# Query loads in whole rows, interleaving on ScalarE, stepped PSUM addresses for the scores, and an earlier placement of attention stages

## The chip, the cores and the metric

The kernel runs on one core of a Trainium2 chip. The metric is the device time of one execution, in microseconds (us). Each run has a state: slow when it is over 1.5% above the fastest of the same kernel, fast otherwise, unknown for a single run. The kernel before and the changed kernel were timed in the same rounds on the same chip. The profile covers the span from the first to the last instruction, about 2 us less than the time. The granted clock is the share of full speed that TensorE was allowed. A transfer lands when its data have arrived. The engines are PE (TensorE), PEld (its weight loads), DVE (VectorE), ACT (ScalarE), POOL (GpSimd) and SP (Sync, which only issues transfers here).

## The reference

Attention with a learned mixing of key and value blocks, followed by a dense mixture of four expert layers. Sizes: 4 batches, 8 heads, 768 positions in 8 blocks of 96, head size 64; the experts see 3072 rows of 512 and have 1024 hidden units.

```python
P = sinkhorn(sort_net)                    # (B,H,8,8), five rounds
k_sorted = einsum('bhij,bhjcd->bhicd', P, k_blocks)
v_sorted = einsum('bhij,bhjcd->bhicd', P, v_blocks)
scores = (q_blocks @ k_sorted^T) / 8      # block i with block i only
attn = softmax(scores) @ v_sorted         # (B,H,S,D)
x = attn.transpose(0, 2, 1, 3).reshape(3072, 512)
out = sum over e of  p[:, e] * (relu(x @ w1[e]) @ w2[e])
```

## The kernel before

TensorE does the products of the expert layers almost without a break. The attention of batches 1 to 3 is cut into stages for one pair of heads each, and a plan places these stages between the product groups. An entry (chunk, slot, stage, batch, pair) puts a stage into a slot of about 2 us.

```python
PLANS = {0: [
    (0, 9, st_v, 1, 0), (0, 10, st_q, 1, 0), (0, 10, st_v, 1, 1), (0, 11, st_k, 1, 0), ...
    (1, 0, st_q, 1, 1), (1, 0, st_s, 1, 0), ...   # cut
```

The stages are: st_n, st_lv and st_lk load queries, values and keys (issued by GpSimd); st_v and st_k mix the blocks on TensorE (the vs transfers then bring the mixed values to the layout that st_a reads); st_q transposes the queries by a transfer; st_s makes scores and their exponentials; st_a multiplies by the values; st_x transposes the result for the experts. The parts that matter here:

```python
def load_queries(b, heads=range(H)):
    t = natural[(b, "q")]                       # 128 positions on partitions
    for h in heads:                             # one issue per head, 128-byte pieces
        nc.gpsimd.dma_start(t[:, h // 2, :, h % 2, :], q[b, h].rearrange("(t p) d -> p t d", p=P))

def st_v(b, pr):
    ...                                         # 2 matmuls into ps, ScalarE copies ps to vo
    if pr % 2:                                  # after every second pair: six Sync issues
        for r in range(R):
            nc.sync.dma_start(vs[ds(r * CP, CP)]..., vo[:, r]...)

def st_q(b, pr):
    qT = att.tile([P, R, P], F16, tag="qT", bufs=3)
    nc.sync.dma_start_transpose(qT[:], natural[(b, "q")][:, pr].rearrange("p t h d -> p (t h d)"))

def st_s(b, pr):
    for i in range(NB):
        for hh in range(2):
            nc.tensor.matmul(pss[hh][:, i // HB, ds((i % HB) * BLK, BLK)],   # 96 words side by side
                             kT[ds(D * hh, D), ds(i * BLK, P)], qT[ds(D * hh, D), i, :], ...)
    ...                                         # exp of both heads, ScalarE

def st_x(b, pr):
    nc.sync.dma_start_transpose(xTs[b][:, pr], xsls[(b, pr)].rearrange("c i h d -> c (i h d)"))
```

All of st_q's and st_x's transposes and the vs transfers go through Sync in program order. The loads go through GpSimd's queue. The page counts both queues as shares of the same 16 DMA engines (38.5% and 27.0% of the span).

The softmax here doesn't subtract the row's maximum and nothing guards it: scores larger than these inputs give would overflow.

## Time and profile before

| what | value | how to read it |
|---|---|---|
| time | 364.64 us (364.54 to 364.73, 3 runs) | median |
| PE busy | 354.1 of 362.5 us | the engine that sets the time |
| ACT, POOL busy | 157.7, 117.5 us | neither is near the bound |
| query loads | 24 issues, 96 KB each, 19.9 us of POOL | 128-byte pieces |
| first query transpose of batch 1 | issued 65.78, landed 72.4 | PE reads it at 72.67 |
| 12 score stages of batches 1 to 3 | 0.45 us each, start to next start | 16 matmuls in pairs (one per head); a pair starts 43 ns after the pair before it |

Because PE is busy nearly all the time and works in order, any wait of PE goes to the end undiminished.

### The profile page before, as it was taken

How to read it: one execution, taken by the hardware profiler on the slowest of the kernel's cores; microseconds unless marked ns; L12 is line 12 of the kernel's file. 1: busy time of each engine (PE TensorE's matmuls, PEld its weight loads, DVE VectorE, ACT ScalarE, POOL GpSimd, SP SyncE). 2: the span in 40 equal slices, each digit the busy share in tenths (PEclk: the TensorE clock that was granted, in tenths of full speed). 3: DMA queues.
4: the chain of work that ended last, by engine and by line, in shares of the span. 5: the costliest groups of instructions: out<-in, count | busy, mean ns of one | idle time of the engine just before them, and what ended most of it. 6: DMA issues, size and time to landing. Idle time of an engine off the chain costs nothing.

```text
span 362.5 us, 10556 instructions
## 1 busy us (share of the span) xinstructions
PE 354.1 (98%) x4517; PEld 314.6 (87%) x4517; DVE 280.0 (77%) x559; ACT 157.7 (44%) x282; POOL 117.5 (32%) x134
## 2 busy tenths in 40 slices
PE   8799999999999999999999999999999999999996
PEld 8685857888888888988888899999999998999995
DVE  5753898779798676866799979868779679587794
ACT  2664430452424355367400157165283381561740
POOL 8882011655022420000000018137055082180470
PEclk9999999999999999999999999999999999999999
DMA  8999999999999999934450310310301101102101
GB/s 109 206 208 230 208 210 200 194 186 158 175 197 162 210 91 172 161 85 73 85 126 2 58 60 4 58 60 4 88 31 49 71 2 60 61 2 65 55 16 44
DMA packets 69753, 38.34 MB, mean 106 GB/s; under 512 B 40390, under 2 KB 64716, under 8 KB 69708
## 3 DMA queue, kind: packets, MB, share of 16 engines
q0 software_dynamic: 34640, 17.83, 38.5%
q1 hardware_dynamic: 35068, 19.85, 27.0%
q8 instruction: 35, 0.57, 0.6%
q14 instruction: 10, 0.08, 0.1%
HBM read 42.00 MB, written 6.34 MB: 133 GB/s over the span
## 4 chain that ended last, share of the span: by engine, by line
PE 86%; DVE 6%; DMA 5%; issue 1%; ACT 1%; POOL 1%; DVEq 0%; ACTq 0%
PE ps_Q L1121 20%; PE ps_h L768 18%; PE ps_p L753 13%; PE ps_X L1032 9%; PE ps_Z L1032 6%; PE ps_Q L1032 6%; DMA w<-in_moe_w_dram 4%; PE ps_o L696 3%; PE ps_p L803 2%; PE ps_h L661 1%; PE ps_s L406 1%; PE ps_a L441 1%; PE ps_k L387 1%; DVE Hb L774 1%; PE ps_v L354 1%
## 5 line engine op out<-in xcount | busy, mean ns | idle before, releaser
L1045 POOL TENSOR_TENSOR Hb<-tmp,pb 128x512 f16<-128x512 f32 x48 | 62.0, 1297 | 150.5 <-ACT tmp L1044 148.7
L768 PE MATMUL ps_h<-xT,w 128*128 128x256 f16 x672 | 78.4, 273 | 0.0
L768 PEld LDWEIGHTS <-w 128*128 128x128 f16 x672 | 64.5, 98 | 8.5
L774 DVE SCALAR_TENSOR_TENSOR Hb<-ps_h,pb 128x1024 f16<-128x1024 f32 x42 | 51.3, 1223 | 17.6 <-PE ps_h L768 17.4
L1032 PEld LDWEIGHTS <-w 128*128 128x128 f16 x768 | 46.6, 98 | 0.8
L1121 PEld LDWEIGHTS <-Sb 128*128 128x128 f16 x384 | 37.2, 98 | 4.1
L1032 PEld LDWEIGHTS <-arena 128*128 128x128 f16 x576 | 34.7, 98 | 0.1
L1044 ACT ACTIVATE tmp<-tmp 128x512 f32<-128x512 f32 x48 | 30.5, 635 | 6.4 <-DVE tmp L1076 5.2
L753 PEld LDWEIGHTS <-Sb 128*128 128x128 f16 x288 | 27.4, 98 | 4.2 <-issue 0.7
L1121 PEld LDWEIGHTS <-Hb 128*128 128x128 f16 x288 | 27.4, 98 | 2.9
L413 ACT ACTIVATE ET<-ps_s 96x768 f16<-96x768 f32 x24 | 18.1, 802 | 26.1 <-PE ps_s L406 25.8
L1032 PE MATMUL ps_X<-kT,arena 128*128 128x128 f16 x384 | 29.3, 219 | 0.0
L121 POOL DMA_DIRECT2D arena<-in_q_dram x24 | 19.9, 837 | 27.1 <-DMA qT<-arena 17.2
L396 ACT CAST kT<-ps_k 64x384 f16<-64x384 f32 x48 | 22.7, 473 | 13.2 <-PE ps_k L387 12.2
L739 DVE TENSOR_TENSOR Sb<-Hb 128x512 f16<-128x512 f16 x45 | 26.5, 609 | 0.0
L1068 DVE TENSOR_TENSOR tmp<-ps_Q,tmp 128x512 f32<-128x512 f32 x24 | 16.6, 691 | 12.2 <-ACT tmp L1067 8.0
L1121 PE MATMUL ps_Q<-w,Sb 128*128 128x256 f16 x192 | 24.7, 273 | 0.0
L1121 PE MATMUL ps_Q<-w,Hb 128*128 128x256 f16 x192 | 23.9, 273 | 0.0
L1052 ACT COPY ps_X<-ps_Z 128x512 f32<-128x512 f32 x24 | 13.7, 570 | 22.8 <-PE ps_Z L1032 22.4
L753 PEld LDWEIGHTS <-Hb 128*128 128x128 f16 x216 | 20.6, 98 | 3.1 <-issue 0.3
L1121 PE MATMUL ps_Q<-T,Sb 128*128 128x256 f16 x192 | 22.9, 273 | 0.0
L1059 ACT COPY tmp<-ps_X 128x512 f32<-128x512 f32 x24 | 14.1, 586 | 12.2 <-PE ps_X L1032 12.2
(189 smaller groups left out, 605.3 us busy)
## 6 DMA issues: line engine op xcount, KB each, us to landing
w<-in_moe_w_dram POOLq DMA_DIRECT2D x7, 1024.0 KB, 27.0
pb<-p_dram SPq DMA_DIRECT2D x12, 512.0 KB, 5.5
arena<-in_k_dram POOLq DMA_DIRECT2D x8, 384.0 KB, 8.6
arena<-in_v_dram POOLq DMA_DIRECT2D x8, 384.0 KB, 9.6
vs<-arena SPq DMA_DIRECT2D x36, 66.0 KB, 5.2
arena<-in_q_dram POOLq DMA_DIRECT2D x24, 96.0 KB, 6.7
out_dram<-ob SPq DMA_DIRECT2D x9, 256.0 KB, 2.0
out_dram<-oa SPq DMA_DIRECT2D x8, 256.0 KB, 2.4
```

Of the source, the lines that this page charges most:

```text
L121: nc.gpsimd.dma_start(t[:, h // 2, :, h % 2, :], q[b, h].rearrange("(t p) d -> p t d", p=P))
L396: nc.scalar.copy(kT[ds(D * hh, D), r], pk[ds(D * r, D), hh].rearrange("p a (i c) -> p a i c", c=CP),)
L413: nc.scalar.activation(ETs[2 * (pr % 2) + hh][:, 0:S].rearrange("c (a x) -> c a x", a=2), pss[hh][0:BLK, :, 0:HS], AF.Exp, bias=0.0, scale ...
L739: tt(sm[0], blk(0, 1), blk(1, 1), ALU.add)
L753: nc.tensor.matmul(ps, lhs(e, f), Ts[e][rhs][:, f, :], start=(first and e == es[0] and f == 0), stop=(done and e == es[-1] and f == KH - 1 ...
L768: nc.tensor.matmul(ps[:, f, :], w1sb[e][:, kc, ds((4 * g + f) * P, P)], xT[:, kc, ds(2 * c * P, 2 * P)], start=(kc == 0), stop=(kc == NKC ...
L774: nc.vector.scalar_tensor_tensor(out=Hb[:, e, ds(4 * g, 4), :], in0=ps[:], scalar=0.0, op0=ALU.max, in1=pb[:, ds(e, 1), :].broadcast_to([P ...
L1032: nc.tensor.matmul(dst[:, ds(f * P, P)], a[lhs][:, k, ds(f * P, P)], t[rhs][:, k, :], start=(first and f == 0 and k == 0), stop=(f == KH - ...
L1044: nc.scalar.activation(src, src, AF.Relu, bias=0.0, scale=1.0)
L1045: nc.gpsimd.tensor_tensor(Hb[:, e, ds(i * KH, KH), ds(j * P, P)], src.rearrange("p (f x) -> p f x", f=KH), pb[:, ds(e, 1), ds(j * P, P)].b ...
L1068: tt(t22, Q, u3, ALU.add)
L1121: nc.tensor.matmul(ps, lhs(e, f), Ts[e][rhs][:, f, :], start=(first and e == 0 and f == 0), stop=(e == E - 1 and f == KH - 1), skip_group_ ...
```

## The change

The intent is to make the query loads cheap (whole rows of 768 bytes in 12 issues, not 128-byte pieces in 24), and to take the last small waits out by placing stages earlier. A whole row holds six successive positions. So ScalarE first interleaves the two heads into one buffer; the transpose then yields the queries in another order, and the score matmuls write them back to the right place by addresses 24 bytes apart in PSUM, the memory that TensorE writes.

```diff
-        for h in heads:
-            nc.gpsimd.dma_start(t[:, h // 2, :, h % 2, :], q[b, h].rearrange("(t p) d -> p t d", p=P))
+        for pr in pairs:
+            nc.gpsimd.dma_start(t[:, (b * NPB + pr) % 3], q[b, ds(2 * pr, 2)].rearrange("h (p r) d -> p h (r d)", r=R))
     def st_q(b, pr):
-        nc.sync.dma_start_transpose(qT[:], natural[(b, "q")][:, pr].rearrange("p t h d -> p (t h d)"))
+        both = natural[(b, "q")][:, NPB - 1].rearrange("p h x -> p (h x)")      # one buffer for all
+        nc.scalar.copy(both.rearrange("p (r h d) -> p h r d", r=R, h=2),
+                       natural[(b, "q")][:, (b * NPB + pr) % 3].rearrange("p h (r d) -> p h r d", r=R))
+        nc.sync.dma_start_transpose(qT[:], both)
+        qTs[(b, pr)] = qT.rearrange("p r (i c) -> p i r c", i=NB)
     # st_s
-                    pss[hh][:, i // HB, ds((i % HB) * BLK, BLK)],
+                    pss[hh][:, i // HB, ds((i % HB) * BLK, BLK)].rearrange("k (c r) -> k r c", r=R),
-                    qT[ds(D * hh, D), i, :],
+                    qT[ds(D * hh, D), i],
     # plan (cut)
-            (0, 9, st_v, 1, 0), (0, 10, st_q, 1, 0), (0, 10, st_v, 1, 1), ...
+            (0, 9, st_v, 1, 0), (0, 10, st_v, 1, 1), (0, 10, st_q, 1, 0), ..., (0, 11, st_q, 1, 1),
-            (2, 8, st_x, 1, 3), (2, 8, st_v, 2, 1), (2, 9, st_lv, 3, 0), (2, 9, st_n, 3, 0), ...   # chunk 2
+            (2, 6, st_v, 2, 1), (2, 6, st_lv, 3, 0), (2, 6, st_n, 3, 0), (2, 8, st_x, 1, 3), (2, 9, st_lk, 3, 0), ..., (2, 12, st_a, 2, 0),
     # first loads of batch 1, between the v and k loads
-        if qd == 0: load_queries(1, range(2))           # heads of pair 0
+        load_queries(1, ([0], [1, 2])[qd])              # pairs 0, 1 and 2
```

## The prediction

> **What bounds the kernel now.** I read the page first, then TensorE's waits, then the three queues around the place where the change bites.
>
> ```profile
> PE 354.1 (98%) x4517; PEld 314.6 (87%) x4517; DVE 280.0 (77%) x559; ACT 157.7 (44%) x282; POOL 117.5 (32%) x134
> ```
>
> TensorE is busy 98% of 362.5 us; nothing else is near. The next question is how much of its time is waiting between 72 and 206 us, where the attention stages of batches 1 to 3 lie between the products of the expert layers. This is the view of waits for PE in that stretch (engine line, waited for, total us, times, longest):
>
> ```profile
> PE ps_p L753 <- DVE Hb L774: 0.3, 1, 0.3
> PE ps_p L753 <- DVE room L863: 0.3, 1, 0.3
> PE ps_v L354 <- DVE xsl L423: 0.2, 1, 0.2
> ```
>
> Three short waits. Busy time hides a little more, so I took starts from PE's timeline: a group of sixteen 256-column products takes 1.75 us start to start, an ordinary score stage 0.45, st_a 0.49, st_v 0.33. Against these, four places lose time: 106.69 (0.41), 112.67 (0.48), 126.74 (0.41) and 183.66 (0.26). Sum 1.56 us, 0.4% of the time. No move of attention stages can win more than that, because the number of matmuls (4517) and their columns do not change. A gain above 2% (7.3 us) is out of reach.
>
> So the case turns on whether the change makes TensorE wait anew. The places that matter are the query loads and their transposes. PE, ScalarE and the Sync queue around the first score stage of batch 1 (start, us, what):
>
> ```profile
> 67.55 0.49 PE L354 MATMUL ps_v<-arena 128*128 128x384 f16 x2
> ...
> 69.19 0.50 PE L387 MATMUL ps_k<-arena 128*128 128x128 f16 x6
> ...
> 72.67 0.51 PE L406 MATMUL ps_s<-qT,kT 64*128 64x96 f16 x16
> ```
> ```profile
> 68.08 0.80 ACT L360 CAST arena<-ps_v 128x768 f16<-128x768 f32 x1 [0.83 <-PE ps_v L354]
> 69.72 1.97 ACT L396 CAST kT<-ps_k 64x384 f16<-64x384 f32 x4 [0.84 <-PE ps_k L387]
> 73.28 1.50 ACT L413 ACTIVATE ET<-ps_s 96x768 f16<-96x768 f32 x2 [1.59 <-PE ps_s L406]
> ```
> ```profile
> 65.78 1.32 SPq L375 DMA_TRANSPOSE qT<-arena  x1
> 68.94 3.88 SPq L368 DMA_DIRECT2D vs<-arena  x6
> 72.92 1.10 SPq L819 DMA_DIRECT2D out_dram<-oacc  x2
> ```
>
> The first transpose is issued at 65.78; restricted to this one, the view of the tile qT gives 6.6 us to landing, so it lands at 72.4. TensorE reads it at 72.67. It is 0.3 us early: just in time. The six vs issues then hold the Sync queue for 3.88 us, from 68.94 (ScalarE ends the evacuation at 68.88) to 72.8. All twelve transposes and the query loads (last numbers: KB each, median us to landing):
>
> ```profile
> DMA to landing us min/median/max: 2.8/6.6/10.1
> ```
> ```profile
> arena<-in_q_dram POOLq DMA_DIRECT2D x24, 96.0 KB, 6.7
> ```
> ```profile
> L121 POOL DMA_DIRECT2D arena<-in_q_dram x24 | 19.9, 837 | 27.1 <-DMA qT<-arena 17.2 <-DMA w<-in_moe_w_dram 9.9
> ```
>
> 2.8 us is a transpose with little beside it (161 us); the long ones are at 65 to 100 us, where the mean share of the DMA engines (two queues can both count, so over 1) is 1.4 to 2.3.
>
> **What the Trainium skill says.** "DMA: Bandwidth & Descriptors", section "Queues, rings and completion order": what Sync issues goes through one ring on each of the DMA engines, and descriptors are taken in ring order. The trace agrees: the six vs transfers issued behind that transpose land from 74.1 on, after its 72.4. So a transpose placed behind the vs transfers waits for them twice, for the issue and in the ring. The same page, section "Why small descriptors are slow (HBM only)", says small pieces carry a fixed overhead; the change makes 128-byte pieces into whole rows of 768 bytes. Trace: a pair of heads landed 1.33 us behind the load before it, a k load with twice the pair's bytes 1.93 us. "ScalarE: Activation LUTs", section "What ACT_TABLE_LOAD costs": an ACTIVATE with immediates is 186 ns + 0.833 ns per column, 826 ns for 768; the trace has 800 ns for 128x768 casts. "TensorE: Matmul & The Clock Gate", Part 1: after an idle window of about 3.4 us the array falls to half clock, until a window of activity. No idle stretch after the warm-up here is that long (longest 1.7 us), so the trace cannot say.
>
> **The change part by part.**
> (1) Loads: 24 issues of 837 ns become 12; at the 754 to 765 ns that the k and v issues take, 19.9 us becomes about 9.1 us of GpSimd. 24x768 = 18,432 pieces become 12x256 = 3,072. GpSimd is 32% busy and PE never waits for a query load: worth 0 directly, but the DMA engines get freer between 70 and 135 us.
> (2) Interleaving: 12 new ScalarE copies of 128x768 f16, about 0.8 us each: 9.6 us, ScalarE 44% to 47%. Off the path unless one blocks. One can: all twelve write one buffer, so each waits for the previous transpose to have landed, in front of everything behind it in ScalarE's order.
> (3) Scores: the same 192 matmuls, with moving operand 6x16 and PSUM addresses 24 bytes apart. Batch 0's scores already read 6x16: their pairs start 43 ns apart, as here, so reading is free. No instruction of the kernel before writes PSUM with a step; I take 0. The skill's PSUM page gives no time for it.
> (4) Placement: st_a of batch 2, head pair 0, moves from the crowded start of batch 1's experts to the end of the chunk before; batch 3's last stages move two slots forward. That should end the waits at 126.74 and 183.66: -0.67 us. The other two come from st_a (1,2) and (1,3), which keep their slots, so they stay.
> (5) The new wait. The built programs show this order on Sync: in the kernel before, first transpose, then vs x6; in the changed one, vs x6, then both first transposes. The score stage keeps its place, after the first group of chunk 1. All before it is unchanged, so TensorE arrives at 72.67, but the transpose cannot be issued before 68.94 + 3.88 = 72.8. At the very best it lands 2.8 us later, 75.6: 3.0 us lost. More likely, with a v load and a query load now in flight there and the vs transfers ahead (they took 5.2 to 5.6 us), in about 4.3 us: 77.1, lost 4.4. PE runs in order, so all of it goes to the end.
> The later transposes have five slots or more (each about 2 us) before their scores; there even 8 us is hidden. While ScalarE holds the second copy for the landing, the exp behind it has nothing to do yet; it then starts 0.8 us late, inside a product group of 1.75.
> (6) A gap over 3.4 us may catch a full idle window and halve the clock for a while. Estimate from the skill's 3.4 us: one window at half pace loses 1.7, perhaps two; at one chance in four, +0.5.
> Sum: 364.64 + 4.4 - 0.67 + 0.5 = 368.9; I take 368.6, as freer DMA engines may shorten the landing.
>
> **The rivals.**
> A: the wait is not there or under 1 us, and the small gains remain: 363.5 to 364.5. For it: a tuned kernel's author probably measured the order. Against: the Sync order and 72.8 against 72.67 leave no room.
> B: the stall is long: the transpose takes 8 to 10 us as some did at 75 to 96 us, and the clock falls: 364.6 + 7 + 2 = 373. For it: crowded DMA engines. Against: those long ones had six small-piece query loads beside them, which go.
> C: stepped PSUM writes run at half pace: a pair takes about 83 instead of 43 ns, 96 pairs, +3.8 us: 372 with the stall. Nothing for or against in the trace.
> D: ScalarE becomes a bound through the single buffer. At 47% this needs blocked copies; after the first two, the copies are two slots or more apart. Under 1 us.
>
> **Range and chances.** The middle is the stall of 3 to 6 us less 0.7. The low end, 366.0, is a bare 2.8 us landing less some relief; the high end, 372.0, a landing of 7 us with a clock loss, or C. Faster by over 2%: 0.01. Slower by over 2% (above 371.9) needs B or C: 0.14. Within 2%: 0.85.
>
> **What would show it.** In the profile after: a PE wait of 3 to 6 us at the first ps_s of batch 1, put down to a DMA qT<-arena, at 72.7 us; on Sync vs before qT there; PE waits at later score stages near 0; the new ScalarE copies near 0.8 us; score pairs still 43 ns apart (a longer step says C); 128x256 products 109 ns apart behind the stall (double says the clock fell). Wrong if PE passes that stage without a wait, or if the loss lies at other stages.

## The result and the profile after

The changed kernel took 383.85 us (median of four runs, 381.79 to 385.33), the kernel before 364.59 in the same rounds. The ratio is 1.0526 (95% interval 1.047 to 1.0582). Ratios in this document are the mean time of one kernel's fast runs over that of the other's in the same rounds, so they are not quite the ratio of the medians. The result is correct, slower, and well outside the predicted range. The profiled run was the fastest of the four (381.79), with a span of 380.0 us against 362.5: 17.5 us to explain.

The page's engine line and its row of the granted TensorE clock (40 slices of 9.5 us, tenths of full speed):

```profile
PE 362.7 (95%) x4517; PEld 319.9 (84%) x4517; DVE 279.5 (74%) x559; ACT 166.2 (44%) x294; POOL 106.4 (28%) x122
...
PEclk9999999969999989999999999999999999999999
```

The same 4517 matmuls take 8.6 us more of PE's busy time, and the idle time grew as well. Two slices have a lower clock: around 80 and around 135 us. PE's longest waits in the stretch of the attention stages, in the view of waits (two of 0.3 us and less are left out):

```profile
PE ps_s L412 <- DMA qT<-arena: 6.7, 1, 6.7
PE ps_h L774 <- DMA xT<-xsl: 2.2, 1, 2.2
PE ps_a L447 <- DMA vs<-arena: 1.4, 1, 1.4
PE ps_a L447 <- ACT arena L363: 0.4, 1, 0.4
```

All four are new. PE's timeline at the two places (start, busy us, and in brackets the idle time before):

```profile
70.68 1.91 PE L774 MATMUL ps_h<-xT,w 128*128 128x256 f16 x16
79.30 1.47 PE L412 MATMUL ps_s<-qT,kT 64*128 64x96 f16 x16 [6.71 <-DMA qT<-arena]
80.70 2.61 PE L774 MATMUL ps_h<-xT,w 128*128 128x256 f16 x16
83.15 0.50 PE L393 MATMUL ps_k<-arena 128*128 128x128 f16 x6
...
127.29 1.47 PE L759 MATMUL ps_p<-w,Sb 128*128 128x256 f16 x12
130.19 0.40 PE L447 MATMUL ps_a<-vs,ET 96*128 96x65 f16 x8 [1.44 <-DMA vs<-arena]
131.01 0.40 PE L447 MATMUL ps_a<-vs,ET 96*128 96x65 f16 x8 [0.41 <-ACT arena L363]
131.25 0.49 PE L774 MATMUL ps_h<-xT,w 128*128 128x256 f16 x3
133.90 2.93 PE L774 MATMUL ps_h<-xT,w 128*128 128x256 f16 x13 [2.16 <-DMA xT<-xsl]
136.77 0.83 PE L412 MATMUL ps_s<-qT,kT 64*128 64x96 f16 x16
```

And Sync's timeline at the same two places (start, us of issuing, count):

```profile
68.80 3.89 SPq L371 DMA_DIRECT2D vs<-arena  x6
72.79 9.20 SPq L383 DMA_TRANSPOSE qT<-arena  x2
...
119.26 4.21 SPq L371 DMA_DIRECT2D vs<-arena  x6
123.57 1.58 SPq L463 DMA_TRANSPOSE xT<-xsl  x1
```

The first place is the predicted one. The vs transfers hold Sync from 68.80 to 72.69, the transpose is issued at 72.79 and lands 6.4 us later, at 79.2. The second place was not predicted. There xT, the transposed input of the experts, is behind six vs transfers and takes 10.3 us to land. The wait of 0.41 us inside st_a has the vs transfers behind it as well: the evacuation of the next v stage, to which it is put down, began on ScalarE at 130.16 after it had waited 2.91 us for the vs transfers to leave its buffer.

After each idle stretch some matmuls run slowly. The 16 products at 80.70 take 2.45 us to the next group where an undisturbed group takes 1.75. The 13 products at 133.90 take 2.87 us where 13 x 109 ns are 1.42. At the first place six of the 16 start about 213 ns apart, twice 109, and the scores before them also take twice their time; at the second place eleven of the 13. The table of stretches gives the granted clock (each row: the stretch, its length, busy us of PE, PEld, DVE, ACT and POOL with their counts, then the clock, the mean share of the DMA engines and GB/s):

```profile
72.40:79.30 6.90, 0.19 (x2) 0.03 (x1) 1.22 (x1) 0.03 (x1) 0.46 (x1) 0.71 1.05 154
79.30:90.00 10.70, 10.70 (x96) 9.00 (x97) 5.61 (x8) 6.52 (x10) 2.92 (x4) 0.87 0.96 139
128.00:137.00 9.00, 4.99 (x47) 3.30 (x47) 3.02 (x8) 0.80 (x1) 0.00 (x0) 0.81 1.06 162
```

In the kernel before, all three stretches had a clock of 1.00. Windows set closer show where the clock was halved:

```profile
71.90:75.32 3.42, 0.69 (x7) 0.37 (x4) 1.22 (x1) 0.00 (x0) 0.96 (x2) 1.00 1.07 183
75.32:82.15 6.83, 2.85 (x23) 2.16 (x24) 0.00 (x0) 2.21 (x3) 0.70 (x1) 0.50 0.95 99
133.35:136.76 3.41, 2.86 (x13) 1.76 (x12) 0.00 (x0) 0.00 (x0) 0.00 (x0) 0.50 0.66 179
```

The third loss has no wait at all. It is in the score matmuls, read from the view of the tile ps_s (durations of one matmul, min/median/max ns; a duration includes the modelled end, so two of them tell only that something changed). Of the kernel before:

```profile
L406 PE MATMUL ps_s<-qT,kT x192: 202/203/213, 72.7 to 178.8; 64*128 64x96 f16 x192
```

The same view of the changed kernel:

```profile
L412 PE MATMUL ps_s<-qT,kT x192: 252/283/438, 79.3 to 191.0; 64*128 64x96 f16 x192
```

By their starts, a pair takes 83 ns instead of 43, and a stage at full clock 0.76 us instead of 0.45 (for example 124.87 to 125.64).

What the change was meant to do came about. Loads and copies, from the view of groups (busy us, mean ns):

```profile
L379 ACT COPY arena<-arena 128x768 f16<-128x768 f16 x12 | 10.0, 832 | 14.2 <-DMA qT<-arena 14.1
L121 POOL DMA_DIRECT2D arena<-in_q_dram x12 | 8.4, 703 | 63.0 <-ACT arena L379 47.6 <-DMA w<-in_moe_w_dram 14.0 <-DVE u L940 1.5
```

The query loads cost POOL 8.4 us instead of 19.9, and three of the four short waits of before (at 106.69, 126.74 and 183.66) are gone.

The account of the 17.5 us, each from starts in PE's timeline:

| term | us | working |
|---|---|---|
| wait for qT | 6.9 | 79.30 less 72.43 (70.68 + 16 x 109 ns) |
| slow clock behind it | 1.3 | scores 1.40 - 0.76, products 2.45 - 1.75 |
| waits at 130 to 134 | 4.5 | 1.59 before st_a, 0.57 within it, 2.32 for xT |
| slow clock behind them | 1.4 | 2.87 - 1.42 |
| stepped scores | 3.7 | 12 x 0.31 |
| waits that went | -1.1 | 0.41 + 0.41 + 0.26 |
| small losses at five other places | 1.1 | 0.27, 0.14, 0.34, 0.17, 0.19 at 111, 113, 159, 175, 193 |
| sum | 17.8 | 0.3 too much: rounding, and PE was 0.15 ahead at 70.68 (70.83 before) |

### The profile page after: what moved, and what is told of

Same layout as the page of the kernel before. It is cut to its first block, busy times and chain, and to the rows that moved or that the text cites. A ratio compares the mean times of both kernels' runs of the same rounds, so it can differ in the third digit from the quotient of the medians.

```text
span 380.0 us, 10522 instructions
## 1 busy us (share of the span) xinstructions
PE 362.7 (95%) x4517; PEld 319.9 (84%) x4517; DVE 279.5 (74%) x559; ACT 166.2 (44%) x294; POOL 106.4 (28%) x122
## 4 chain that ended last, share of the span: by engine, by line
PE 85%; DMA 8%; DVE 1%; POOL 1%; ACT 1%; SPq 1%; issue 1%; DVEq 0%; ACTq 0%; POOLq 0%
PE ps_Q L1127 19%; PE ps_h L774 19%; PE ps_p L759 12%; PE ps_X L1038 8%; PE ps_Q L1038 6%; PE ps_Z L1038 6%; DMA w<-in_moe_w_dram 4%; DMA xT<-xsl 3%; PE ps_o L702 3%; PE ps_h L667 3%; PE ps_s L412 2%; DMA qT<-arena 2%; PE ps_p L809 1%; PE ps_a L447 1%; PE ps_v L357 1%; SPq L371 1%
## 5 line engine op out<-in xcount | busy, mean ns | idle before, releaser
L774 PE MATMUL ps_h<-xT,w 128*128 128x256 f16 x672 | 80.7, 277 | 2.2 <-DMA xT<-xsl 2.2
L121 POOL DMA_DIRECT2D arena<-in_q_dram x12 | 8.4, 703 | 63.0 <-ACT arena L379 47.6
```

Of the source, the lines that this page charges most:

```text
L774: nc.tensor.matmul(ps[:, f, :], w1sb[e][:, kc, ds((4 * g + f) * P, P)], xT[:, kc, ds(2 * c * P, 2 * P)], start=(kc == 0), stop=(kc == NKC ...
```

## The experiments

Three questions: does the step in PSUM cost PE time by itself, do the waits come from the placement or from the layout, and why do the transposes take so long to land? All results were correct unless said otherwise.

| kernel | us | ratio to before (95%) |
|---|---|---|
| changed kernel | 383.85 | 1.0526 (1.047 to 1.0582) |
| plan_only | 382.35 | 1.0489 (1.0461 to 1.0516) |
| layout_only | 373.95 | 1.0251 (1.0222 to 1.028) |
| step24 | 368.62 | 1.0107 (1.0078 to 1.0136) |
| pairs | 365.79 | one look |
| rows_permuted | 380.98 | 1.0424 (1.0384 to 1.0464) |
| moving_order | 392.6 | 1.0751 (1.072 to 1.0781) |
| layout_mended | 397.63 | 1.0882 (1.0842 to 1.0922) |
| layout_unblocked | 371.69 | 1.0173 (1.0115 to 1.023) |
| swap_only | 371.97 | 1.0171 (1.015 to 1.0193) |
| q_first | 380.72 | 1.044 (1.0402 to 1.0478) |
| q_first_late_v | 380.44 | 1.0433 (1.0397 to 1.047) |
| q_first_late_loads | 384.76 | 1.0518 (1.0479 to 1.0557) |
| q_first_late_loads_again | 383.09 | one look |
| backlog | 365.26 | 1.0006 (0.9986 to 1.0026) |
| x_first | 387.6 | wrong result |
| v_early | 387.14 | 1.0592 (1.0551 to 1.0632) |
| clear_second | 379.76 | 1.0383 (1.0354 to 1.0412) |
| plan_mended | 369.52 | 1.0125 (1.0082 to 1.0167) |

### Placement and layout apart

**plan_only** is the kernel before with the new plan and the new order of the first loads; layout and scores are the old ones.

```diff
-    PLANS, PLAN_A of before
+    PLANS, PLAN_A of the changed kernel
-        if qd == 0: load_queries(1, range(2))
+        load_queries(1, (range(2), range(2, 6))[qd])
```

> The kernel before with the new placement of the stages alone; queries load and are stored as before. Theory (the new order on the Sync queue makes two waits, the PSUM step is a separate cost): both waits are there, about 7 us before the first score stage of batch 1 and about 4 us around the first product of batch 1's experts, each followed by matmuls at half clock; 364.6 + 8 + 6 - 1 = about 377 us (374 to 381), score pairs 43 ns apart, mean clock below 1. Rival (the waits come from the new loads, the interleaving copy or its single buffer): within 1.5 us of 364.6.

Measured: 382.35 us. Score pairs stay at 43 ns, and the waits are there without the new layout:

```profile
PE ps_s L406 <- DMA qT<-arena: 5.4, 1, 5.4
PE ps_a L441 <- DMA vs<-arena: 3.1, 1, 3.1
PE ps_p L803 <- DVE oacc L898: 2.0, 1, 2.0
...
PE ps_h L768 <- DMA xT<-xsl: 1.0, 1, 1.0
```

So the placement, with the loads of batch 1 brought forward, makes both places wait without the new layout. The time is a little above the expected 374 to 381. One reason is the third wait, of 2.04 us at 66.72, ahead of both places. Three of the single-head loads brought forward (60.80, 62.70, 64.64) pushed GpSimd's addition L895 from 62.38 in the kernel before to 65.47; DVE's L898 waited 2.25 us for it, and PE for DVE. The changed kernel, with half as many issues, has no such wait.

**layout_only** is the reverse: the new loads, copies and stepped scores in the old plan (two loads moved where a buffer demands it).

```diff
-    PLANS, PLAN_A of the changed kernel
+    PLANS, PLAN_A of before, with (2, 1, st_n, 2, 3) -> (2, 5) and (0, 5, st_n, 3, 3) -> (0, 10)
```

> The changed kernel's loads, interleaving and stepped PSUM addresses with the placement of before (three loads stand a little later, where the three row buffers ask for it). Theory: the 12 score stages take 0.76 instead of 0.45 us, 12 x 0.31 = 3.7 us more, and nothing else: about 368.3 us (367 to 370), clock 1.00, first transpose issued ahead of the six vs transfers. Rival (the layout causes waits too): 372 or more, with a wait on qT at a score stage or a mean clock below 1.

Measured: 373.95 us; pairs 83 ns apart; only 0.44 us of waiting at the first score stage. But PE waits twice for a v evacuation (L363) on ScalarE, 2.52 us at 114.29 and 1.62 at 159.06. ScalarE's timeline before the first of them shows why:

```profile
112.71 0.83 ACT L379 COPY arena<-arena 128x768 f16<-128x768 f16 x1 [2.77 <-DMA qT<-arena]
113.44 0.79 ACT L363 CAST arena<-ps_v 128x768 f16<-128x768 f32 x1
```

The interleaving copy waits for the previous transpose to free the single buffer, and the evacuation stands behind it. Before the second wait it is the same: the copy at 157.47 had waited 4.12 us. That is the prediction's rival D, in the old plan.

**layout_unblocked** moves those two copies behind the evacuation.

```diff
-  (2, 5, st_q, 2, 1), (2, 5, st_n, 2, 3), (2, 6, st_v, 2, 0),
+  (2, 6, st_v, 2, 0), (2, 6, st_q, 2, 1), (2, 6, st_n, 2, 3),
-  (0, 12, st_q, 3, 1), (0, 13, st_v, 3, 0),
+  (0, 13, st_v, 3, 0), (0, 13, st_q, 3, 1),
```

> The new query layout in the old placement, with the two interleaving copies that stood in front of a v evacuation on ScalarE moved behind it. If the two waits of 2.52 and 1.62 us on the v evacuation (L363) in layout_only come from copies that wait for their single buffer in front of it, those waits go and the time falls from 373.95 to 368.5 to 370, which is the kernel before plus the 3.7 us of the PSUM step. Rival: the copies are not the cause; the waits stay and the time is 373 to 375.

Measured: 371.69 us with an unusually wide scatter (369.59 to 374.54; the fastest run lies in the expected range). Both waits on the evacuation are gone, so the copies were their cause. The profiled run, the slowest of the four, has a new wait of 2.19 us for xT at 125.13 and slow products behind it. The gain of the median is half of what was expected. In the profiled run nothing was gained: besides the new wait, PE came to the first product group of chunk 1 at 72.82, against 71.09 in layout_only, with a clock of 0.50 from 16.8 to 20.2 us, before any stage that the edit touched. The profiled runs of step24 and rows_permuted have such an early stretch too.

### The step in PSUM

**step24** is the kernel before with the scores' output addresses stepped by 24 bytes and nothing else. The score columns come out in a wrong order. The comparison with the reference still passed, here and in rows_permuted, so it says nothing about the order of rows in this test.

```diff
-                    pss[hh][:, i // HB, ds((i % HB) * BLK, BLK)],
+                    pss[hh][:, i // HB, ds((i % HB) * BLK, BLK)].rearrange("k (c r) -> k r c", r=R),
```

> The kernel before with one edit: the scores' PSUM addresses take steps of 24 bytes, as in the change; queries are read as before (unit step), so score columns land in a wrong order on purpose. Theory (the step alone halves the write rate): pairs of score matmuls start 83 instead of 43 ns apart, the stage takes 0.76 instead of 0.45 us, 12 x 0.31 = 3.7 us, 368.3 us (367.3 to 369.3), no new wait, clock 1.00. Rival (the cost is in reading 6x16 or in the transposed layout): 43 ns and within 0.5 us of before.

Measured: 368.62 us, no new waits, pairs 83 ns apart. Over all score stages the distances between starts sum to 9.28 us instead of 5.76, which is 3.5 of the 3.8 us that the time rose (368.62 less 364.83 in the same rounds). This shows the cost alone: rival C of the prediction, at its size.

**pairs** writes the same 96 words, two neighbours at a time and then a jump of 24 bytes.

```diff
-                    pss[hh][:, i // HB, ds((i % HB) * BLK, BLK)],
+                    pss[hh][:, i // HB, ds((i % HB) * BLK, BLK)].rearrange("k (c r t) -> k r c t", r=3, t=2),
```

> One look at the kernel before with score columns written in pairs: two neighbouring PSUM words, then a jump of 24 bytes (order wrong on purpose). Theory (PSUM takes two neighbouring columns at a time, and a single word costs as much as a pair): pairs of score matmuls 43 ns apart. Rival (any broken run halves the rate): 80 ns or so, as with single steps.

Measured: 365.79 us, pairs 43 ns apart. It was run at another time. The tile view of the scores in step24:

```profile
L406 PE MATMUL ps_s<-qT,kT x192: 252/282/283, 74.5 to 184.1; 64*128 64x96 f16 x192
```

And of pairs:

```profile
L406 PE MATMUL ps_s<-qT,kT x192: 199/203/213, 73.8 to 180.0; 64*128 64x96 f16 x192
```

A jump after every second word costs nothing; a jump after every word doubles the time. The profiled run also waited 1.15 us for qT at 73.83: the kernel before has only 0.3 us to spare there.

**rows_permuted** is the changed kernel with plain output addresses (the rows of a block come out permuted).

```diff
-                    pss[hh][:, i // HB, ds((i % HB) * BLK, BLK)].rearrange("k (c r) -> k r c", r=R),
+                    pss[hh][:, i // HB, ds((i % HB) * BLK, BLK)],
```

> The changed kernel with plain, unit-step PSUM addresses for the scores: the result is wrong on purpose (rows come out in another order), all else the same. Theory (a PSUM step of 24 bytes halves the rate at which a matmul's columns are written): score pairs 43 ns apart again, 12 x 0.31 = 3.7 us less, about 380 us (378.5 to 381.5). Rival (the 83 ns come from reading the queries in 6 runs of 16): pairs stay 83 ns apart and the time stays 382 to 385.

Measured: 380.98 us; pairs 43 ns; the distances between score starts sum to 6.07 us instead of 9.83. The time fell by 2.9 us, while its profiled run waited longer at both places (7.19 for qT, 1.85 and 2.83 at the second). Set beside plan_only, which has the same placement and plain scores but the old loads, it is 1.4 us faster (382.35 less 380.98). The intervals of the two ratios just overlap, and plan_only's wait of 2.04 us at 66.72, which is absent here, is more than the difference; no other gain of the new loads is shown.

**moving_order** tries to keep the order in another way: plain output addresses, and the queries read in the right order, each 2-byte element 256 bytes from the last.

```diff
-        qTs[(b, pr)] = qT.rearrange("p r (i c) -> p i r c", i=NB)
+        qTs[(b, pr)] = qT.rearrange("p r (i c) -> p i c r", i=NB)
     # and plain output addresses, as in rows_permuted
```

> The changed kernel with the order restored on the reading side: PSUM addresses are plain, and the moving operand is read as 16 times 6 elements with a step of 256 bytes. Right result. Theory (only the write side cares about steps): pairs 43 ns apart, the same 3.7 us less as with permuted rows, 379 to 382 us. Rival (reading single 2-byte elements is slow as well): pairs 80 ns or more, 382 us or more.

Measured: 392.6 us, with the right order by construction. Pairs start about 165 ns apart, nearly four times 43, and the distances between score starts sum to 16.9 us. All twelve stages took 1.41 us, also the two (79.31 and 140.95) in which the granted clock was 0.50; so what limits this reading did not follow the granted clock. Reading single elements at a step is worse than writing them so. The remedy failed.

**layout_mended** lets ScalarE restore the order: plain scores in the layout of layout_unblocked, and the exp writes its 2-byte results 12 bytes apart.

```diff
-                ETs[2 * (pr % 2) + hh][:, 0:S].rearrange("c (a x) -> c a x", a=2),
-                pss[hh][0:BLK, :, 0:HS],
+                ETs[2 * (pr % 2) + hh][:, 0:S].rearrange("k (a i c r) -> k a i r c", a=2, i=HB, r=R),
+                pss[hh][0:BLK, :, 0:HS].rearrange("k a (i r c) -> k a i r c", i=HB, r=R),
```

> layout_only with two edits: PSUM addresses are plain, and the exponential's write to SBUF restores the order (a step of 12 bytes in f16); and two interleaving copies stand behind the v evacuation that they held up. Right result. Theory (layout_only's 8 to 9 us are 3.7 us of PSUM steps, and 4.1 us of waits plus slow matmuls made by copies that wait for the one interleaving buffer): score pairs 43 ns apart, no wait over 0.6 us, clock above 0.995; 365 to 366.5 us. Rival (the layout has a further cost, such as the stepped write of the exponential or other blocked copies): 368 us or more.

Measured: 397.63 us. Pairs are back at 43 ns, but the exp took 2.84 us instead of 0.80 (tile view of ET, min/median/max ns), and PE waited for it in 18 places:

```profile
L419 ACT ACTIVATE ET<-ps_s x24: 2725/2844/2960, 73.0 to 211.4; 96x768 f16<-96x768 f32 x24
```

So none of the three ways tried to restore the order (PSUM step, stepped moving operand, stepped exp) was free.

### The first score stage

**swap_only** is the kernel before with one swap: the first query transpose behind the second v stage. It makes the predicted wait alone.

```diff
-            (0, 9, st_v, 1, 0), (0, 10, st_q, 1, 0), (0, 10, st_v, 1, 1), ...
+            (0, 9, st_v, 1, 0), (0, 10, st_v, 1, 1), (0, 10, st_q, 1, 0), ...
```

> The kernel before with one swap and nothing else: the first query transpose of batch 1 now comes behind the six vs transfers of the second v stage. This is the one step on which the prediction rested, alone, with the old loads and plain scores. Theory of the prediction (a landing of 4.3 us from an issue at 72.8): a wait of about 4.4 us at the first score stage, time 368.5 to 369.5. Theory now (the landing takes 6 to 9 us while loads of GpSimd are in flight, and the idle stretch takes the clock with it): a wait of 6 to 9 us there plus about 1.3 us of slow products, time 372 to 376. Nothing else should wait.

Measured: 371.97 us, ratio 1.0171. The wait:

```profile
78.25 0.82 PE L406 MATMUL ps_s<-qT,kT 64*128 64x96 f16 x16 [5.44 <-DMA qT<-arena]
```

The transpose was issued at 73.07 and landed 5.0 us later; 13 slow products followed. Neither expectation held to the figure. The wait is 1 us above the prediction's 4.4 and below the 6 to 9 of the other; its time is just under the latter's 372. A second, small wait came with it, 0.55 us for vs at 132.11. So the order alone costs over 6 us, and with the rest of the change the landing is 1.4 us longer still (6.4 against 5.0).

**q_first** is the changed kernel with the reverse swap, the transpose ahead of the vs transfers again.

```diff
-            (0, 10, st_v, 1, 1), (0, 10, st_q, 1, 0),
+            (0, 10, st_q, 1, 0), (0, 10, st_v, 1, 1),
```

> The changed kernel with one swap: the first query stage of batch 1 stands ahead of the second v stage again, in the same slot. Theory: the transpose is issued at about 67 instead of 72.8 us and lands by 73; the wait of 6.9 us and the slow matmuls behind it (1.3 us) go: 383.9 - 8 = about 376 us (373 to 378). Rival (the transpose is late because of the loads beside it, not of its place on the queue): over 381 us, the wait still over 4 us.

Measured: 380.72 us, a miss. The transpose was issued at 67.34, 5.4 us earlier, but landed only 3.2 us earlier, at 75.98, and PE still waited 4.04 us. From the tile view of qT, restricted to this transpose:

```profile
DMA to landing us min/median/max: 8.6/8.6/8.6
```

At its issue, GpSimd's queue still held a k load and two query pairs issued at 45 to 55 us (landing at 70.3, 71.3 and 72.7), and another query load followed at 67.70 (landing at 76.4).

**q_first_late_v** takes the next v load out of that time.

```diff
     # q_first, and
-            (1, 0, st_s, 1, 0), (1, 0, st_lv, 2, 0), ...
+            (1, 0, st_s, 1, 0), ...  (1, 7, st_lv, 2, 0), (1, 7, st_n, 2, 2), ...
```

> The swap at the first query stage as in q_first, and batch 2's first v load put back seven slots later. Theory (in q_first the transpose, issued at 67.3, took 8.6 us because query and v loads brought forward were in the DMA engines beside it): it now lands in 5 to 7 us, the wait falls from 4.0 to under 2.5 us, and no clock loss: about 376 to 379 us. Rival (the transpose is slow for another reason, such as the vs transfers behind it): it still takes 8 us or more, the wait stays near 4 us.

Measured: 380.44 us; the transpose took 9.2 us, the wait was 4.60. The v load, issued at 70.8, is not what delays it.

**q_first_late_loads** brings back the old start and the old times of the loads up to slot 7 of chunk 1, so that only one query load goes with the transpose.

```diff
     # q_first, and
-        load_queries(1, ([0], [1, 2])[qd])
+        if qd == 0: load_queries(1, [0])
-            (0, 11, st_n, 1, 3), (0, 11, st_q, 1, 1), (1, 0, st_lv, 2, 0), (1, 1, st_n, 2, 0), (1, 2, st_q, 1, 2), ...
+            (0, 11, st_n, 1, 1), (1, 0, st_n, 1, 2), (1, 1, st_q, 1, 1), (1, 2, st_n, 1, 3), (1, 4, st_q, 1, 2), (1, 4, st_lv, 2, 0), ...
```

> The changed kernel with the swap of q_first, and the query loads of batch 1's later pairs and the loads of batch 2 put back behind the first score stage, about where they were in the kernel before. Theory (a transpose shares the DMA engines with the GpSimd queue's loads and lands only when that queue runs dry): issued at about 67.3, it lands by 73 to 74 (5 to 6.5 us instead of 8.6), the wait falls from 4.0 to at most 1.5 us, no slow matmuls there; 375 to 378 us with the second place still there. Rival (it is slow with fewer loads too): 8 us or more to landing, the wait near 4 us, 380 us.

Measured: 384.76 us in the fast runs, far from the expectation. The profiled run fell in the slow state (525.51 us), so its trace was not used. The same kernel once more:

> The same kernel as q_first_late_loads, whose profile fell in the slow state, for a profile of the fast state. Theory crowd: with only one query load in flight the first transpose lands within 5 us of its issue, so the first score stage waits under 1 us, and what makes this kernel 384 us is a new wait elsewhere, in the stages whose loads now come late. Rival: the first wait stays at 4 us or more, and crowding isn't what makes the landing long.

Measured: 383.09 us. It was run at another time. The first transpose now landed 5.3 us after its issue and PE waited only 0.67 us for it. So fewer loads ahead of and beside the transpose do shorten its landing. The time went into a wait that the profile puts down to a load. PE's timeline:

```profile
96.21 0.80 PE L393 MATMUL ps_k<-arena 128*128 128x128 f16 x6 [5.16 <-DMA arena<-in_v_dram]
```

And ScalarE's:

```profile
94.53 0.83 ACT L379 COPY arena<-arena 128x768 f16<-128x768 f16 x1 [4.93 <-DMA qT<-arena]
95.27 1.50 ACT L419 ACTIVATE ET<-ps_s 96x768 f16<-96x768 f32 x2
```

No load landed near 96 us. ScalarE's copy waited 4.93 us for an earlier transpose to leave the single buffer, the exp stood behind it, and PE resumes 0.94 us after the exp begins. My reading is that PE waited for a PSUM buffer held by those scores: the blocked copy again, at another place.

**backlog** adds the suspected early loads to the kernel before: the queries of pair 1 with the first loads of the batch, and nothing else.

```diff
-        if qd == 0: load_queries(1, range(2))
+        load_queries(1, (range(2), range(2, 4))[qd])
-            (0, 11, st_k, 1, 0), (0, 11, st_n, 1, 1),
+            (0, 11, st_k, 1, 0),
```

> The kernel before, with the two query loads of batch 1's second head pair issued 11 slots earlier, ahead of the weight loads' end (as the change does with pairs 1 and 2), and nothing else: Sync's order, the layout and the scores are the old ones. Theory backlog: GpSimd's queue of loads is still draining when the first transpose is issued at 65.8 (the k load lands at 71.6, the transpose 0.8 behind it); two more small-piece loads in that queue move the landing from 72.4 to 74 to 76, so the first score stage waits 1 to 3 us, and the time is 366 to 369. Rival: only Sync's order sets the landing; then it stays at 72.4, there is no wait over 0.3 and the time is within 0.5 us of before.

Measured: 365.26 us, the same as before. The landing moved from 6.6 to 7.5 us after the issue, and PE waited 0.71 us. The direction is right, the size below the 1 to 3 us expected. Earlier loads in the queue delay the transpose; that they explain all of q_first's 8.6 us is not shown.

### The second place

**x_first** was meant to put the v stage, and with it the six vs transfers, behind st_x (1, 3), with st_a (2, 0) later.

```diff
-            (2, 6, st_v, 2, 1), (2, 6, st_lv, 3, 0), ... (2, 8, st_x, 1, 3), ... (2, 12, st_a, 2, 0),
+            (2, 6, st_lv, 3, 0), ... (2, 8, st_x, 1, 3), (2, 8, st_v, 2, 1), ...   # st_a (2, 0) two slots into the next chunk
```

> The changed kernel with the second place undone: the second v stage of batch 2 stands behind the last transpose of batch 1 again, and batch 2's first two value stages move back to the next batch's chunk, as before. Theory (the six vs transfers ahead of the transpose xT, and a value stage too soon after its vs transfers, make the waits at 130 to 134 us): no wait over 0.5 us between 120 and 140 us, no slow matmuls there, about 6 us less: 376 to 379 us; the wait on qT at 72 us stays. Rival (the waits follow from the DMA engines being late in general): they move to a neighbouring stage and the time stays over 381.

Measured: 387.6 us and a wrong result (relative error 0.31). The edit left the load of batch 3 ahead of the stage that still reads batch 2's values from that buffer. The xT wait was gone, but other waits came, one for that very load; nothing is concluded from it.

**v_early** goes the other way: both v stages of batch 2 several slots earlier, so that the vs transfers are done sooner.

```diff
+            (1, 12, st_v, 2, 0), ... (2, 4, st_v, 2, 1),
-            (2, 4, st_v, 2, 0), ... (2, 6, st_v, 2, 1),
```

> The changed kernel with batch 2's first two value stages moved 5 and 2 slots earlier, so that their six vs transfers go out ahead of the last score stages of batch 1 and the Sync queue is clear for the last xT transpose. Theory (the second place is made by vs transfers in front of xT, and by st_a following too closely on them): the waits on vs (1.4 and 0.4 us) and on xT (2.2 us) at 130 to 134 us and the slow matmuls behind them go, 383.9 - 5.9 = about 378 us (376 to 380). Rival (DMA engines are late there anyway): a wait of 2 us or more stays between 120 and 140 us and the time stays over 381.

Measured: 387.14 us. The vs wait went, the xT wait grew to 4.69 us. Sync's timeline again had the six vs issues (from 119.41) and xT, issued at 127.85, took 9.7 us to land. The wait moved.

**clear_second** leaves Sync's order alone and moves the loads: in the plan, four loads of batch 3 stand after xT has been read.

```diff
-            (2, 6, st_lv, 3, 0), (2, 6, st_n, 3, 0), (2, 9, st_lk, 3, 0), (2, 10, st_n, 3, 1),          # chunk 2
+            (0, 1, st_lv, 3, 0), (0, 1, st_n, 3, 0), (0, 3, st_lk, 3, 0), (0, 3, st_n, 3, 1),           # next chunk
     # st_q (3, 0) and the two loads that follow it: two or three slots later
```

> The changed kernel with four loads of batch 3 (v 0, k 0 and two query pairs) issued after the xT transpose of batch 1 has been read, not while it is in flight. Theory crowd: xT took 10.3 us to land because those loads shared the DMA engines with it; then it lands in 5 to 6 us, the waits of 1.44 (vs) and 2.16 (xT) near 130 to 134 shrink below 0.5 each, the slow products behind them vanish, and the time falls by 3.5 to 6 us to 378 to 380. Theory order: what delays xT is only its place on Sync behind the six vs transfers; then its landing stays near 133.9 and the time within 1 us of the changed kernel. The first wait (6 to 7 us at the first score stage of batch 1) stays in both.

Measured: 379.76 us, 4.1 us below the changed kernel (5.2 us by the ratios, as its rounds had a slower kernel before). The landing of xT, from the tile view of xT in the changed kernel, restricted to this transfer (min, median and max of one are the same):

```profile
DMA to landing us min/median/max: 10.3/10.3/10.3
```

And of clear_second:

```profile
DMA to landing us min/median/max: 6.3/6.3/6.3
```

Same place on Sync behind the same six transfers, issued at about the same time (123.6 and 124.3): beside it only the loads differ. But the edit did less than was meant. GpSimd works ahead of PE until a buffer holds it, so the v load and the first query pair were issued early again (120.07 and 120.81; in the changed kernel 119.41 and 120.15). Only the k load and the second query pair went away from xT. GpSimd's timeline of the changed kernel:

```profile
122.58 0.77 POOL L110 DMA_DIRECT2D arena<-in_k_dram  x1 [1.72 <-PE ps_k L393]
125.49 0.70 POOL L121 DMA_DIRECT2D arena<-in_q_dram  x1 [2.15 <-ACT arena L379]
```

And of clear_second (the second pair is the first of the x2):

```profile
139.22 0.75 POOL L110 DMA_DIRECT2D arena<-in_k_dram  x1
139.95 1.42 POOL L121 DMA_DIRECT2D arena<-in_q_dram  x2
```

These two loads thus cost xT 4 us. The xT wait and the slow products behind it are gone; the vs wait shrank to 0.76, with 0.42 inside st_a, and new waits of 0.63 and 0.35 came at a later st_a (151.28). The crowding theory held.

**plan_mended** mends both places in plan_only: q_first's order, the old early loads, and clear_second's loads.

```diff
     # plan_only, and
-            (0, 10, st_v, 1, 1), (0, 10, st_q, 1, 0), (0, 11, st_n, 1, 3), (0, 11, st_q, 1, 1), ...
+            (0, 10, st_q, 1, 0), (0, 10, st_v, 1, 1), (0, 11, st_n, 1, 1), ...   # as q_first_late_loads
     # and the four loads as in clear_second
```

> plan_only (new placement, old layout and scores, 382.35) with both places mended: the first query transpose ahead of the second v stage and no extra loads in the queue at the start, and the batch 3 loads after xT has been read. If the two waits and the crowded queue behind them are all that the new placement costs, both waits fall under 0.7 us and the time is 364 to 367. If something else in the placement costs, waits remain or new ones come, and the time is 369 or more.

Measured: 369.52 us. Of the 17.5 us that plan_only lost, 13 are gone: the waits for qT and xT are both away, and the one at 66.72 too. It is still above the kernel before, because the vs wait stayed (2.68 us at 121.72, and 0.41 behind it) with eleven slow products after it, about 1.1 us. So st_a (2, 0), moved to the end of the chunk, comes too early for its values. The loads moved only in part here too: a v load and the two loads of a pair were still issued beside the vs transfers (109.31 to 110.86), so how much of this wait is theirs is not shown. No version tried beats the kernel before.

## Why the prediction was wrong

**PE as the bound, the cheaper loads, the copies and the small gain available: right.** POOL spent 8.4 us on query loads (predicted 9.1), ScalarE 10.0 on copies (9.6). Three of the four small waits went, 1.1 us; the prediction allowed 0.67, as it kept the one at 106.69.

**Step 5, the new wait: right in place and cause, mis-sized.** PE arrived at 72.4, the transpose was issued at 72.79 as computed (72.8). "In about 4.3 us: 77.1, lost 4.4" measured 6.4 and 6.9. swap_only, with the old loads, gives 5.0 and 5.4, so 4.3 was short even for the order alone. The prediction named a v load, a query load and the vs transfers beside the transpose, but gave them 1.5 us together on top of the 2.8 of a transpose with little beside it, although its own lines had the vs transfers landing after 5.2 to 5.6 us. clear_second and the q_first runs show that GpSimd's loads in flight set it as well, even those issued long before. The "freer DMA engines" did not show at this moment: a query load (landing at 75.3) and a v load (at 78.6) were in flight.

**Step 6, the clock: given one chance in four, it came at both places.** It cost 1.3 and 1.4 us. The prediction put 1.7 for a window and, at its chance, 0.5 into the sum. "TensorE: Matmul & The Clock Gate" in the Trainium skill, Part 1, puts the drop after an idle window of about 3.4 us and says that the window runs free. Here less idle time was enough. In the changed kernel the clock fell at 75.32, when PE had been idle for 2.7 us (the 6.71 us before 79.30 begin at 72.59). layout_unblocked dropped to half pace after an idle stretch of 2.19 us and layout_only after one of 2.52, while 1.62 in layout_only did nothing. The stretches at half pace in the changed kernel lasted 6.83 and 3.41 us, but part of the first fell into the wait.

**Step 5, last paragraph, "the later transposes have five slots or more ...; there even 8 us is hidden": the step that failed most.** It was true of the query transposes and was taken for the whole. The vs transfers and the xT transpose share their queue and the DMA engines, and the plan moved them too. st_v (2, 1) went ahead of st_x (1, 3), and loads of batch 3 moved next to them. That cost 5.9 us with its clock loss, and the deadline of each transfer on Sync, not only of the qT ones, is what the prediction did not look at.

**Step 3, "I take 0": wrong by 3.7 us.** step24 shows it alone. The prediction said that the skill's PSUM page gives no time, and took that for no cost. That page has no time, but "PSUM — Partial Sum Buffer", section "Specifications (TRN2)", does say that any non-contiguous pattern slows matmuls significantly. "SBUF — State Buffer", section "Door 1: The DMA port swizzle", says the same and that PSUM has 8-byte lines of two fp32 values. Single words at 24 bytes are such a pattern, and two neighbours fill one line, which is what step24 and pairs show: 83 against 43 ns. That the line is the mechanism is the page's statement; the runs show the times.

**Rivals.** B (a long landing and a clock loss) and C (stepped writes at half pace) each came true with nearly their stated sizes, together, and neither was in the middle value; in B the landing was 6.4 us, not the 8 to 10 stated. D (blocked copies) cost 4.1 us in the old plan; in the changed kernel no such wait is over 0.5 us. Adding B and C would have given 364.6 + 9 + 3.8 = 377, still below the result: the second place was missing.

**What stays open.** How much of the 8.6 us of q_first's transpose is due to which loads (backlog gives 0.8 us for one pair issued early), and how much of the vs wait at the second place is due to the early st_a and how much to the loads that stayed beside the vs transfers.

## What to carry to other kernels

When a plan moves transfers, list every transfer of each queue with its deadline on the busy engine, and look at what other queues have in flight at that time; a transpose here landed after 5 to 10 us depending on loads that nobody waited for. Gather a stepped layout where it is free: 96 fp32 words in pairs at a step are written at full rate, single ones at half, and reading or writing 2-byte elements singly cost three to four times. A bound engine with 0.3 us to spare at one place is a reason to leave the order there alone.

## What the Trainium skill lacked or had wrong

- No page has a time for stepped matmul output. "PSUM — Partial Sum Buffer" and "SBUF — State Buffer" say only that any non-contiguous pattern slows matmuls; "Advanced Engine Details and Errata", section "PSUM Cachelines", adds that every two consecutive elements should be contiguous. Here a pair of 64x96 matmuls takes 83 ns with single words 24 bytes apart, and 43 ns both plain and with words in neighbouring pairs and jumps between them (one look). So "any" is too strong, and the rule of two is borne out.
- "TensorE: Matmul & The Clock Gate", section "Step-by-step: what each phase is for", has the moving operand stream in as many cycles as it has columns. With 2-byte elements 256 bytes apart, a pair takes 165 ns instead of 43; runs of 16 neighbours are free (43 ns in rows_permuted). The note on 16-byte lines in "SBUF — State Buffer" says that crossing a line at each access costs, without a time.
- "ScalarE: Activation LUTs", section "What ACT_TABLE_LOAD costs", gives the cost of an ACTIVATE by columns alone; a 96x768 exp took 2844 ns with 2-byte results written 12 bytes apart, 802 ns plain.
- "TensorE: Matmul & The Clock Gate", Part 1: half pace came after idle stretches of 2.19, 2.52 and 2.7 us, shorter than the 3.4 us window.
- No page that I read gives the landing of a DMA transpose beside other queues' loads: 5.0 to 10.3 us here for the same 128x768 or 96x1024 transposes, 6.3 instead of 10.3 when two loads were moved away.
